# Three raw weight pieces requested two rounds later in an attention and feed-forward kernel

## The chip, the cores and the metric

The kernel runs on one core of one Trainium2 chip. The metric is the device time of one execution in microseconds (us); lower is better. The core has five engines with instruction streams of their own: TensorE (PE, matrix products), VectorE (DVE), ScalarE (ACT), GpSimd (POOL) and SyncE (SP), which here only issues DMA transfers. 16 DMA engines move the data. An engine takes its instructions in the order in which they were written.

## The reference

An attention with a threshold, followed by a feed-forward layer with a softmax-weighted activation and a layer norm:

```python
# q, k, v: (8, 8, 576, 64) float32; tau: a number
scores = matmul(q, k^T) / sqrt(64)
thresh = max(scores, -1) - tau
scores = where(scores >= thresh, scores, -1e9)
attn   = softmax(scores)                     # with 1e-9 in the sum
x      = matmul(attn, v), heads side by side # (4608, 512)
# w_in: (512, 1024), w_out: (1024, 512): float64; g_ln: (1024): float32
h    = x @ w_in
solu = h * softmax(h)
ln   = (solu - mean) / sqrt(var + 1e-6) * g_ln
out  = ln @ w_out                            # (4608, 512) float32
```

w_in and w_out arrive as 8-byte floats. The kernel reads them as pairs of 32-bit words and builds 4-byte floats from them itself.

## The kernel before, in words

**Rounds.** The loop at the end of the kernel runs in rounds (`rnd`), one for each of 144 slots, and some more to finish. A slot is half of a pair of heads. In the round of slot s, PE computes the scores (`s_ps`, L400), DVE takes the row maximum and a masked copy (`maxes`, L421, giving `nth`), and ACT applies the threshold ramp (L436) and the exponential (L445). One round later POOL normalises (L452 to L455), and DVE transposes the weights block by block into `T` (L467, in `blocks`). After every second slot, SP issues three DMAs that move `T` to `wT` (L476 and twice L478). Some rounds later PE multiplies `wT` by v (`pv`, L508) and ACT copies the result into `xh` (L538). When four pairs of heads are ready, PE multiplies `xh` by w_in (`h_ps`, L571), DVE takes the row maximum (`hm`, L586), and so on through the layer norm to the product with w_out (`o_ps`, L676). The texts write wT5, wT7, wT9, wT11, wT13 for the `wT` of the unit whose second slot is 5, 7, 9, 11, 13.

The order on every engine is the order in which Python calls the instructions, without rearrangement.

**Weight pieces.** w_in and w_out are cut into 16 raw pieces of 128 rows x 512 columns x 8 bytes = 512 KB: 0 to 7 are w_in, 8 to 15 w_out. `weight_load` (L248) asks SP for one. Piece x is converted in round x - 1: `weight_e` takes the exponent bits (DVE L258, then ACT L263, and L266 for w_out), `weight_m` the mantissa bits (DVE L274), `weight_b` puts them together (DVE L290 and L295), `weight_c` multiplies on POOL (L305) a round later. `weight_e(x + 1)` and `weight_m(x + 1)` run in the round of piece x, so the first read of piece x + 1 falls there. `weight_d` (L313) asks SP for two transfers that swap halves of converted w_out pieces.

**Which buffer.** The list `RAW` gives each piece a buffer that is otherwise used later: pieces 6 and 12 share `xh2`, 7 and 13 `xh3`, 8 and 14 `uT`. A load into such a buffer waits until DVE has read the piece that lay in it.

**When a piece is asked for.** The table `ASK` says which load is issued behind the conversion of which piece:

```python
weight_b(x)
for y in ASK.get(x, ()):
    weight_load(y)
```

In each round this stands after `blocks`, so after that round's `wT` transfers on SP, and before `weight_d` and the loads in `load_at` (v, q and k of this and the next batch).

Of the kernel before, what the change touches and what calls it, by code (L numbers as in the profile page):

```python
# [20 lines left out]
def kernel(  # L21
# [216 lines left out]
    third = heads.tile([P, S], F32, tag="kT", name="third")[:, 0:512].bitcast(I32)  # L238

    RAW = ['xh2', 'xh3', 'uT', 'xh1', 'u', 'V', 'xh2', 'xh3', 'uT', 'xh1', 'u', 'V', 'xh2', 'xh3', 'uT', 'xh2']  # L240
    ASK = {0: [6], 1: [7], 2: [8], 3: [9], 4: [10], 5: [11], 6: [12], 7: [13], 8: [14], 12: [15]}

    def weight_load(x, queue=None):
        raw = work.tile(
            [P, 512], I64 if wide else F32, tag=RAW[x],
            bufs=1, name="raw"
        )
        (queue or nc.sync).dma_start(out=raw, in_=piece(x)[0])  # L248
        raws[x] = dict(raw=raw)
# [29 lines left out]
    def weight_b(x, part=2):  # L279
        d = raws[x]  # L280
        _, dst, unit = piece(x)
        if not wide:
            if part != 1:
                nc.vector.tensor_scalar(out=dst, in0=d["raw"], scalar1=unit, scalar2=None, op0=ALU.mult)
            return
        words = d["raw"].bitcast(I32).rearrange("p (n two) -> p n two", two=2)
        lo, hi = words[:, :, 0], words[:, :, 1]
        if part != 1:
            m = d["m"]
            nc.vector.scalar_tensor_tensor(  # L290
                out=dst, in0=lo.bitcast(U32), scalar=2.0**-32, in1=m, op0=ALU.mult, op1=ALU.add
            )
        if part != 0:
            e = d["e"]
            nc.vector.scalar_tensor_tensor(  # L295
                out=e, in0=hi, scalar=-(2**31), in1=e, op0=ALU.bitwise_and, op1=ALU.bitwise_xor
            )
# [477 lines left out]
    with tc.manual_schedule():  # L775
# [45 lines left out]
        while True:  # L821
# [145 lines left out]
            if rnd in pieces:  # L967
# [4 lines left out]
# [3 lines that stand above are left out]
# [43 lines left out]
```

## Time and profile before

| | |
|---|---|
| median of 3 runs | 853.83 us (853.14 to 856.76) |
| profiled execution | 854.08 us, of which the span is 852.3 us |
| PE busy | 818.3 us (96%) |
| DVE busy | 680.2 us (80%) |
| ACT busy | 572.2 us (67%) |
| POOL busy | 499.1 us (59%) |
| DMA | 168.54 MB, mean 198 GB/s |
| chain that ended last | PE 82%, DVE 5%, DMA 5%, ACT 3% |
| mean granted TensorE clock | 0.985 |

The profile is one execution. Busy times are shares of the whole span; a stage can be bound by another engine than the whole. "Idle before <- X" names what ended an engine's idle time. A matmul's end is modelled, so a busy PE is not PE at its peak. Issue instructions of DMAs are not counted as busy; the SP queue view lists them with the time each took to issue.

### The profile page before, as it was taken

How to read it: one execution, taken by the hardware profiler on the slowest of the kernel's cores; microseconds unless marked ns; L12 is line 12 of the kernel's file. 1: busy time of each engine (PE TensorE's matmuls, PEld its weight loads, DVE VectorE, ACT ScalarE, POOL GpSimd, SP SyncE). 2: the span in 40 equal slices, each digit the busy share in tenths (PEclk: the TensorE clock that was granted, in tenths of full speed). 3: DMA queues.
4: the chain of work that ended last, by engine and by line, in shares of the span. 5: the costliest groups of instructions: out<-in, count | busy, mean ns of one | idle time of the engine just before them, and what ended most of it. 6: DMA issues, size and time to landing. Idle time of an engine off the chain costs nothing.

```text
span 852.3 us, 36109 instructions
## 1 busy us (share of the span) xinstructions
PE 818.3 (96%) x15363; PEld 619.0 (73%) x15363; DVE 680.2 (80%) x1241; ACT 572.2 (67%) x1127; POOL 499.1 (59%) x945
## 2 busy tenths in 40 slices
PE   5769899999999999999999999999999999999997
PEld 4547678677677787666687777777777777777555
DVE  5999977889788888888788878888888888787361
ACT  5888876877676666666676666677666677775121
POOL 3888756665566656565566666565666655555120
PEclk9779999999999999999999999999999999999999
DMA  9999887898888788887888887887889877655212
GB/s 332 271 252 220 214 217 202 209 240 211 220 220 215 192 200 209 214 211 180 206 234 208 198 182 196 231 211 196 191 225 226 207 183 187 156 136 139 66 38 63
DMA packets 75314, 168.54 MB, mean 198 GB/s; under 512 B 11146, under 2 KB 32658, under 8 KB 75154
## 3 DMA queue, kind: packets, MB, share of 16 engines
q1 hardware_dynamic: 74866, 165.82, 77.2%
q8 instruction: 120, 1.97, 1.0%
q10 hardware_dynamic: 288, 0.43, 0.2%
q14 instruction: 40, 0.33, 0.1%
HBM read 46.14 MB, written 9.44 MB: 65 GB/s over the span
## 4 chain that ended last, share of the span: by engine, by line
PE 82%; DVE 5%; DMA 5%; ACT 3%; issue 2%; POOL 1%; SPq 1%; DVEq 0%; ACTq 0%; POOLq 0%
PE o_ps L676 27%; PE h_ps L571 23%; PE s_ps L400 15%; PE pv L508 14%; DMA wT<-T 3%; PE h_ps L561 3%; DVE w L421 2%; DVE T L467 1%; ACT w L436 1%; ACT w L445 1%; DMA raw<-in_moe_w_in_dram 1%; DVE w L290 0%; POOL w L455 0%; SPq L478 0%; POOL sm L453 0%
## 5 line engine op out<-in xcount | busy, mean ns | idle before, releaser
L676 PE MATMUL o_ps<-w,uT 64*64 64x256 f32 x4608 | 269.3, 376 | 2.2 <-issue 1.9
L436 ACT ACTIVATE w<-s_ps,nth 128x576 f32<-128x576 f32 x280 | 196.9, 737 | 106.6 <-DVE nth L421 85.1
L676 PEld LDWEIGHTS o_ps<-w,uT 64*64 64x64 f32 x4608 | 226.8, 133 | 50.3 <-ACT xh L538 11.6
L421 DVE CUSTOM_DVE_ANT_0 w<-s_ps,tau_t 128x576 f32<-128x576 f32 x280 | 199.9, 750 | 77.6 <-PE s_ps L400 48.4
L455 POOL TENSOR_SCALAR w<-w,sm 128x576 f32<-128x576 f32 x288 | 221.9, 782 | 14.3
L467 DVE STREAM_TRANSPOSE T<-w 128x576 f32<-128x576 f32 x288 | 207.7, 755 | 22.7 <-POOL w L455 21.2
L571 PE MATMUL h_ps<-w,xh 64*64 64x512 f32 x1856 | 219.6, 589 | 0.0
L445 ACT ACTIVATE w<-w,ntau 128x576 f32<-128x576 f32 x288 | 219.5, 766 | 0.0
L508 PEld LDWEIGHTS pv<-wT,v 64*64 64x64 f32 x5760 | 170.5, 135 | 36.7 <-issue 22.2
L400 PE MATMUL s_ps<-kT,qT 64*64 64x64 f32 (+1 forms) x2048 | 173.6, 413 | 16.0 <-ACT w L436 13.5
L508 PE MATMUL pv<-wT,v 64*64 64x128 f32 (+1 forms) x5760 | 172.2, 262 | 5.0 <-DMA wT<-T 4.9
L571 PEld LDWEIGHTS h_ps<-w,xh 64*64 64x64 f32 x1856 | 113.0, 133 | 82.2 <-issue 54.4
L452 POOL TENSOR_SCALAR sm<-sm 128x2 f32<-128x2 f32 x144 | 36.1, 251 | 188.2 <-ACT w L445 184.8
L453 POOL TENSOR_TENSOR sm<-sm,mone 128x2 f32<-128x2 f32 x144 | 107.6, 747 | 12.0
L400 PEld LDWEIGHTS s_ps<-kT,qT 64*64 64x64 f32 x2048 | 71.5, 136 | 24.9 <-ACT w L436 18.5
L538 ACT COPY xh<-pv 128x256 f32<-128x256 f32 x64 | 25.4, 396 | 74.6 <-PE pv L508 74.6
L637 ACT ACTIVATE V<-u,nb,rs 128x1024 f32<-128x1024 f32 x36 | 44.7, 1241 | 40.6 <-POOL nb L627 34.4
L663 DVE STREAM_TRANSPOSE uT<-V 128x1024 f32<-128x1024 f32 x36 | 44.1, 1225 | 14.5 <-DMA V<-u 13.9
L445 ACT ACTIVATION_READ_ACCUMULATOR w<-w,ntau 128x1 f32 x288 | 55.3, 192 | 0.0
L601 DVE TENSOR_TENSOR u<-h_ps,u 128x1024 f32<-128x1024 f32 x36 | 42.8, 1190 | 9.9 <-ACT u L595 9.9
L642 DVE TENSOR_SCALAR u<-u,rs,nb 128x1024 f32<-128x1024 f32 x36 | 34.9, 969 | 17.5 <-ACT V L637 17.4
L595 ACT ACTIVATE u<-h_ps,hm 128x1024 f32<-128x1024 f32 x36 | 40.1, 1115 | 9.9 <-DMA V<-u 5.6
(81 smaller groups left out, 565.4 us busy)
## 6 DMA issues: line engine op xcount, KB each, us to landing
wT<-T SPq DMA_DIRECT2D x160, 288.0 KB, 6.5
wT<-T SPq DMA_DIRECT2D x64, 576.0 KB, 5.5
v<-in_v_dram SPq DMA_DIRECT2D x16, 576.0 KB, 4.9
V<-u SPq DMA_DIRECT2D x144, 64.0 KB, 3.5
out_dram<-ob SPq DMA_DIRECT2D x71, 128.0 KB, 2.7
q<-in_q_dram SPq DMA_DIRECT2D x28, 288.0 KB, 5.9
k<-in_k_dram SPq DMA_DIRECT2D x27, 288.0 KB, 6.1
qT<-flip SPq DMA_DIRECT2D x48, 144.0 KB, 3.4
```

The source lines that it names most:

```text
L400: nc.tensor.matmul(out=ps[h][ROWS[y], ks], lhsT=lhsT, rhs=d["kT"][ROWS[h], ks], start=True, stop=True,)
L421: nc.vector.tensor_tensor_reduce(out=w, in0=ps[:, 0:S], in1=(zero if loose else tau_t).to_broadcast([P, S]), scale=1.0, scalar=BIG, op0=AL ...
L436: nc.scalar.activation(out=d["w"][x], in_=d["w"][x] if d["loose"] else d["ps"][x][:, 0:S], func=AF.Prelu, bias=d["nth"][x], scale=-1.0, al ...
L445: nc.scalar.activation(out=w, in_=w, func=AF.Exp, bias=ntau, scale=1.0, accum_out=sm[:, x : x + 1])
L453: nc.gpsimd.tensor_tensor(out=sm, in0=sm, in1=mone, op=ALU.pow)
L455: nc.gpsimd.tensor_scalar(out=w, in0=w, scalar1=sm[:, x : x + 1], scalar2=1.0, op0=ALU.mult, op1=ALU.mult)
L467: nc.vector.transpose(out=T[:, :, r, h, :], in_=w)
L508: nc.tensor.matmul(out=to, lhsT=d["v"][ROWS[u], (h0 + h - u) % 4, m,], rhs=rhs, start=m == 0, stop=m == NK - 1,)
L571: mm = nc.tensor.matmul(out=h[ROWS[y], f], lhsT=x[ROWS[r], c, ROWS[y]], rhs=w1_parts[ROWS[r], c, part ^ r], start=part == 0 and c == 0, st ...
L637: nc.scalar.activation(out=V, in_=u, func=AF.Identity, bias=nb, scale=rs)
L663: nc.vector.transpose(out=uT, in_=d["V"].rearrange("p y (m x) -> p m y x", x=32))
L676: nc.tensor.matmul(out=d["o"][ROWS[z], 512 * (r ^ other) : 512 * (r ^ other) + 256], lhsT=d["uT"][ROWS[r], m].rearrange("p y x -> p (y x)" ...
```

## The change

Pieces 12, 13 and 14 are asked for behind the conversions of pieces 8, 9 and 10 (rounds 7, 8 and 9) instead of those of 6, 7 and 8 (rounds 5, 6 and 7). Their buffers, their conversions, the rounds of these and all other loads stay as they are.

```diff
-    ASK = {0: [6], 1: [7], 2: [8], 3: [9], 4: [10], 5: [11], 6: [12], 7: [13], 8: [14], 12: [15]}
+    ASK = {0: [6], 1: [7], 2: [8], 3: [9], 4: [10], 5: [11], 8: [12], 9: [13], 10: [14], 12: [15]}
```

The order of instructions on PE, DVE, ACT and POOL is the same in both kernels. On SP the order around the three loads changes from "11, 12, v, wT5, 13, 14, wT7" to "11, v, wT5, 12, wT7, 13, 14".

## Prediction, made before the changed kernel was run

> **What bounds the kernel now.** I read the page's 40 slices first: how full each engine is over the span. Each digit is the busy share of 21.3 us in tenths.
>
> ```profile
> PE   5769899999999999999999999999999999999997
> DVE  5999977889788888888788878888888888787361
> ```
>
> VectorE (DVE) is the full engine in slices 2 to 5 and TensorE (PE) from slice 6 on. The change works between 38 and 73 us. So I asked next for busy times by stage there; the columns are stage, length, busy us of PE, weight loads, DVE, ACT, POOL, then granted clock, DMA share, GB/s.
>
> ```profile
> 40.00:62.00 22.00, 13.63 (x208) 9.71 (x208) 21.28 (x45) 19.29 (x39) 18.22 (x24) 0.77 1.00 252
> 62.00:74.00 12.00, 11.12 (x170) 8.04 (x174) 11.54 (x24) 10.37 (x20) 10.91 (x16) 1.00 0.84 207
> 74.00:92.00 18.00, 17.05 (x386) 13.04 (x380) 17.78 (x34) 14.75 (x32) 15.56 (x24) 1.00 1.02 230
> ```
>
> DVE is idle for 0.72 us of the 22, 0.46 of the 12 and 0.22 of the 18: it sets the pace of all three stages, and the DMA engines are saturated beside it (1.00). Third, the chain of waits in time order, which says otherwise for ten microseconds:
>
> ```profile
> 55.38 7.90 DMA wT<-T
> ...
> 63.32 2.03 PE pv L508 x65
> ...
> 70.89 3.46 PE h_ps L571 x32
> 74.37 1.23 DVE hm L586
> ```
>
> The chain comes off DVE, through the transfer of the transposed weights wT of slots 6 and 7 (I write wT7), into PE, and back to DVE at 74.37. Fourth, SyncE's (SP's) queue, where the change is made: start, duration, line, transfer, count.
>
> ```profile
> 37.53 3.30 SPq L248 DMA_DIRECT2D raw<-in_moe_w_out_dram  x2
> 40.88 1.61 SPq L151 DMA_DIRECT2D v<-in_v_dram  x3
> 44.08 0.60 SPq L476 DMA_DIRECT2D wT<-T  x1
> ...
> 48.04 2.81 SPq L248 DMA_DIRECT2D raw<-in_moe_w_out_dram  x2
> 54.10 0.58 SPq L476 DMA_DIRECT2D wT<-T  x1
> 54.73 2.85 SPq L478 DMA_DIRECT2D wT<-T  x2
> 58.90 1.30 SPq L313 DMA_DIRECT2D w<-w  x2
> ...
> 64.16 0.60 SPq L476 DMA_DIRECT2D wT<-T  x1
> ```
>
> By the order in the code the pairs of L248 are pieces 11 and 12 (37.53 and 40.50), then 13 and 14 (48.04 and 50.52). Last, who needs what: PE's two pv groups, DVE's first reads of pieces 12, 13 and 14, and the DMA share per microsecond after wT of slots 8 and 9 (wT9).
>
> ```profile
> 62.20 0.44 PE L508 MATMUL pv<-wT,v 64*64 64x128 f32 x4 [2.48 <-DMA wT<-T]
> ...
> 73.95 2.23 PE L508 MATMUL pv<-wT,v 64*64 64x128 f32 x70
> ```
>
> ```profile
> 64.02 0.79 DVE L258 TENSOR_SCALAR em<-raw 128x512 int32<-128x512 int32 x1
> ...
> 69.04 0.68 DVE L258 TENSOR_SCALAR em<-raw 128x512 int32<-128x512 int32 x1
> ...
> 75.51 0.42 DVE L258 TENSOR_SCALAR third<-raw 128x512 int32<-128x512 int32 x1
> ```
>
> ```profile
> 70.00:71.00 1.00, 1.00 (x16) 0.61 (x11) 1.00 (x3) 0.97 (x4) 0.91 (x3) 1.00 0.33 78
> 71.00:72.00 1.00, 1.00 (x14) 0.64 (x10) 1.00 (x4) 0.48 (x1) 0.82 (x3) 1.00 0.10 20
> ```
>
> PE waits 2.48 us and then 0.68 for wT7; for wT9 it does not wait. At 70.4 the DMA backlog is gone, and the engines idle 0.67 + 0.90 = 1.57 us.
>
> **The change, part by part.** No compute instruction is added, removed or moved; three 512 KB loads stand later in SP's queue.
>
> *Where they go.* The order on SP becomes: piece 11, the v loads, wT5, piece 12, wT7, pieces 13 and 14, the weight shuffles of L313, the k loads, wT9. A moved load no longer waits for a conversion, since the piece whose buffer it takes was converted two rounds earlier. So 12 starts at about 48.04, 13 and 14 at 57.6 to 59.2, when SP is through with wT7 (54.73 + 2.85 = 57.58).
>
> *Pieces in time for DVE?* In this trace a raw piece lands 5.9 to 9.4 us after its issue (median 7.6). Piece 12: by 57.4, needed 64.02. Piece 13, issued by 58.2: 64 to 67.6, needed 69.04, at least 1.4 us to spare. Piece 14, issued by 59.2: by 68.6, needed 75.51. Cost 0; the cover of 13 is the thinnest, and each microsecond past 69.04 would be one of the kernel, since DVE is the pace.
>
> *SP's queue.* Behind 13 and 14 stand the shuffles, four k loads and wT9. SP now waits 58.90 - 57.58 = 1.32 us for POOL before the shuffles. Two issues of 0.33 to 0.97 each are 0.66 to 1.94, so the shuffles start 0 to 0.6 later; SP then has 1.01 us free between the k loads' end (60.24 + 2.91) and wT9 (64.16, released by DVE). Cost 0. The removed wait before 40.88 lets the v loads go about 2 us sooner; nobody waits for them.
>
> *wT7 sooner.* It no longer queues behind 13 and 14. Its last transfer took 7.90; the least of any wT before 120 us is 4.4, wT9's took 5.5 to 5.9. So it lands at 59.8 to 61.3 instead of 63.28; I take 60.5, near wT9's figure: 2.8 us. What of it reaches the end? PE's h_ps matmuls start sooner, but the second h_ps stands behind scores that wait for ACT, and ACT for DVE. DVE's step at 74.37 (hm) follows a transpose that ends at 72.77 + 1.50 = 74.27. Gain: 0.10 us; the rest turns into PE waiting for DVE. The most it could be is 0.46, all of DVE's idle time from 62 to 74.
>
> *wT9 later.* The bytes of 40 to 70 us are the same, so wT9 is later by the time the DMA engines run dry on the way. Taking 13 and 14 out of the queue before 54.10 removes 1.05 MB, at 252 GB/s 4.2 us of work. Piece 14, issued at 50.52 with the pair's 7.7, landed near 58.2, so 1.5 to 3.5 us of that work lay beyond 54.10 and was cover. Dry time: 0.7 to 2.7, I take 2.0, the upper half, because piece 12 goes alone. wT9 landed about 64.80 + 5.9 = 70.7; now 71.4 to 73.4, centre 72.7. PE's pv wants it at 73.95: 1.25 us to spare (0.55 to 2.55), and the scores behind that pv end 0.6 us before DVE wants them (76.03 + 1.23 against 77.86). Cost 0.
>
> [...]
>
> *Later on.* Of the 2.0 us, 1.57 fall into the trough at 70.4 to 72 and 0.63 into the one at 88 to 89 (share 0.37). wT11 (issued 76.87, its halves landing in 7.7) has 2 us to spare before its pv at 88.55. wT13 carries the chain at 95.80; it gets 0 to 0.5 later, I take 0.1. From 100 us on PE is full and the order unchanged: what is shifted stays shifted.
>
> Sum: -0.10 + 0.1 = 0. The profiled execution took 854.08 us (span 852.3 and 1.78 around it), 0.25 above the median of 853.83. I forecast the median, 853.9.
>
> **Rivals.**
>
> *Slower: the backlog moves to wT9.* If the queue of 4.5 MB between wT7 and wT9 (two raws, shuffles, k loads, both wT) drains at 207 GB/s, the row of 62 to 74, instead of 252, it takes 21.8 us from 54.7 and wT9 lands at 76.5. It decides beyond 74.55 (73.95 + 0.6): PE stands 2.5 us, DVE loses about 2, and wT13 is late too by up to 1: 856 to 857. For it: wT5 took 9.3 in its halves behind a raw and three v loads. Against: 207 contains the 1.57 us trough. If piece 13 is also late for 69.04, which would take 11 us, two more: about 859.
>
> *Faster: PE is the path from 63 to 74, as the chain says.* Then the 2.8 us of wT7 count: 851.0. For it: PE is full from 63.3 to 86. Against: DVE's own rows leave 0.46 us idle. DVE rows also stretch (0.79 for L258 against 0.42), and if these follow PE's timing, the gain could pass 4 us; little speaks for it.
>
> *A half-clock stretch falls elsewhere.* The granted clock was 0.50 from 54.6 to 58.0, after PE had idled from 49.7 to 52.4, and 1.00 after the like idle from 59.7 to 62.2. If such a 3.4 us falls onto h_ps at 65 to 74, PE loses 1.7 us and DVE's hm 1.6: 855.5. The change fills PE's idle time, which speaks against it. [...]
>
> The edit not doing what it says is excluded by the order on SP, which differs in just these loads.
>
> **How the numbers follow.** Forecast 0.62 (852.8 to 855.3: the bounds -0.46 and +0.5 and the spread of the runs); slower 0.20; faster 0.13; clock 0.05. About 0.5%, 4.3 us, is what a measurement of this kernel can tell from no change; nearly every case lies inside. Beyond it I put half of the slower case, 0.10, for two delays together, and 0.06 of the faster. Same 0.84. The range takes in the rivals' main prices and leaves out what lies beyond them: 851.0 to 857.4.
>
> **What would show it.** Right: wT7's pv starts near 60.5 with PE's wait of 2.48 gone or under 1; hm stays within 0.5 us of 74.37; DMA share dips between 51 and 55 and the trough at 71 shrinks; pv of wT9 shows no DMA wait. Wrong: hm near 72, or DVE idle before a read of raw at 69, or a pv at 74 to 96 waiting for wT a microsecond longer than now.

## The result and the profile after

The changed kernel is slower: a median of 858.07 us (854.79 to 866.6, 18 runs) beside 855.63 us (852.39 to 860.2, 18 runs) for the kernel before, run in turn with it. The two medians are 2.4 us apart; the ratio over all of these runs is 1.0045, with a 95% interval of 1.0026 to 1.0065, so about 3.9 us. Two executions among the experiments below, one of 1431.9 us and one of 984.3, ran at a far lower granted clock (0.56 and 0.85 over the whole execution) and are left out of the ratios given there. The forecast was 853.9 with 0.84 on "no change"; the measured median lies 0.7 us above the range. Part of that distance is the level: the three runs that the forecast started from had a median 1.8 us below the 855.63 of the eighteen.

Single executions of one kernel differ by more than the two kernels do, so one profile cannot show this loss by itself. The first profile of the changed kernel took 854.79 us with a span of 853.0, only 0.7 above the 852.3 of before. It still answers most of the steps of the prediction. First the busy share in 40 slices, which is nearly the same picture as before:

```profile
PE   6669899999999999999999999999999999999997
DVE  6999977889788888888788888888888888777361
```

Next the three stages (stage, length, busy us of PE, weight loads, DVE, ACT, POOL, then granted clock, DMA share, GB/s), and single microseconds with the same columns:

```profile
40.00:62.00 22.00, 14.35 (x232) 9.27 (x236) 20.91 (x44) 19.75 (x38) 18.71 (x24) 0.84 0.92 229
62.00:74.00 12.00, 12.00 (x164) 9.08 (x160) 10.24 (x21) 9.39 (x20) 9.52 (x14) 0.86 1.01 257
74.00:92.00 18.00, 16.99 (x384) 12.85 (x374) 17.80 (x34) 14.45 (x30) 15.69 (x25) 1.00 0.95 227
```

```profile
51.00:52.00 1.00, 0.65 (x10) 0.31 (x12) 1.00 (x2) 1.00 (x4) 1.00 (x2) 0.82 0.49 142
52.00:53.00 1.00, 1.00 (x10) 0.31 (x4) 1.00 (x3) 0.83 (x3) 0.85 (x2) 0.50 0.20 70
53.00:54.00 1.00, 1.00 (x24) 1.00 (x22) 1.00 (x3) 0.82 (x2) 0.92 (x2) 0.50 0.48 105
...
71.00:72.00 1.00, 1.00 (x16) 0.62 (x10) 1.00 (x4) 0.71 (x2) 0.90 (x2) 1.00 1.11 235
```

The DMA engines now run partly dry at 51 to 54 us (shares 0.49, 0.20 and 0.48), and the trough that lay at 71 to 72 (0.10 before) is full (1.11). DVE's loss in this profile is in the middle stage: 10.24 of 12 us busy, where it was 11.54. The clock there is 0.86, where it was 1.00. SP's queue shows the edit (start, duration, line, transfer, count):

```profile
46.04 0.93 SPq L248 DMA_DIRECT2D raw<-in_moe_w_out_dram  x1
52.40 0.57 SPq L476 DMA_DIRECT2D wT<-T  x1
53.02 2.92 SPq L478 DMA_DIRECT2D wT<-T  x2
55.98 2.05 SPq L248 DMA_DIRECT2D raw<-in_moe_w_out_dram  x2
...
59.47 3.68 SPq L142 DMA_DIRECT2D k<-in_k_dram  x4
63.27 0.60 SPq L476 DMA_DIRECT2D wT<-T  x1
64.83 1.89 SPq L478 DMA_DIRECT2D wT<-T  x2
```

Piece 12 goes alone at 46.04, pieces 13 and 14 at 55.98, behind wT7. The pv groups on PE, and two steps of DVE (start, duration, instruction, count, and in brackets the idle time ahead of it and what ended it):

```profile
60.03 0.44 PE L508 MATMUL pv<-wT,v 64*64 64x128 f32 x4 [2.01 <-DMA wT<-T]
61.36 3.44 PE L508 MATMUL pv<-wT,v 64*64 64x128 f32 x66 [0.90 <-DMA wT<-T]
...
73.66 2.22 PE L508 MATMUL pv<-wT,v 64*64 64x128 f32 x70
```

```profile
66.03 0.76 DVE L421 CUSTOM_DVE_ANT_0 w<-s_ps,tau_t 128x576 f32<-128x576 f32 x1 [1.32 <-PE s_ps L400]
...
74.07 1.22 DVE L586 TENSOR_REDUCE hm<-h_ps 128x1 f32<-128x1024 f32 x1
```

PE still waits for wT7, 2.01 + 0.90 us, though the two raw pieces are behind it now. Its pv then took 3.44 us at half clock (0.50 granted from 62 to 65 us) instead of 2.07, and DVE waited 1.32 us for the scores behind it. At wT9 (73.66) PE does not wait in this execution. The hm of DVE is 0.30 us sooner than before, but this execution was further ahead earlier: DVE's step on slot 4 starts at 28.98 us here and at 30.71 in the profile of before.

**The second profile of the changed kernel shows the loss** (861.79 us, span 860.0). Its chain of waits in time order, SP's queue, then PE and DVE:

```profile
59.29 7.58 DMA w<-w
66.86 0.02 issue
66.88 9.87 DMA wT<-T
76.75 0.04 issue
76.79 2.82 PE pv L508 x65
```

```profile
57.34 1.85 SPq L248 DMA_DIRECT2D raw<-in_moe_w_out_dram  x2
59.29 1.30 SPq L313 DMA_DIRECT2D w<-w  x2
...
65.97 2.09 SPq L478 DMA_DIRECT2D wT<-T  x2
```

```profile
75.42 0.44 PE L508 MATMUL pv<-wT,v 64*64 64x128 f32 x4 [1.72 <-DMA wT<-T]
76.79 2.91 PE L508 MATMUL pv<-wT,v 64*64 64x128 f32 x66 [0.94 <-DMA wT<-T]
```

```profile
81.47 0.76 DVE L421 CUSTOM_DVE_ANT_0 w<-s_ps,tau_t 128x576 f32<-128x576 f32 x1 [4.62 <-PE s_ps L400]
```

Read from the end: DVE stands still for 4.62 us at the scores of slot 13. They stand on PE behind a pv that waited 1.72 + 0.94 us for wT9. wT9's last transfer was issued at 66.88 and took 9.87 us. In the profile of before it is the second of the two transfers in this line:

```profile
64.80 2.93 SPq L478 DMA_DIRECT2D wT<-T  x2
```

There it was issued at 65.45 and took 6.30. (A transfer has landed when the last of its 16 semaphore increments is on record; landing times below are read from these.) The trace puts the issue at 66.88 behind the landing of a shuffle (w<-w), itself 7.58 us in flight behind pieces 13 and 14. wT9 does not read that shuffle. What ties the two is a semaphore: SP's 696 transfers use eight semaphores in turn, and none was issued before the eighth ahead of it had landed. The first profiles of before and after show that for 685 of 688 transfers each, and of the other three not all 16 increments are on record. The eighth ahead of wT9's last transfer is this shuffle, in both kernels; it landed at 66.86 here, 0.02 us ahead of the issue, and at 64.34 in the first profile of before, 1.11 ahead.

### The profile page after: what moved, and what is told of

The parts are those of the page before. It is cut to its first block, busy times and chain, and to the rows that moved or that the text cites. A ratio compares the mean times of both kernels' runs of the same rounds, so it can differ in the third digit from the quotient of the medians.

```text
span 853.0 us, 36106 instructions
## 1 busy us (share of the span) xinstructions
PE 818.4 (96%) x15363; PEld 622.5 (73%) x15363; DVE 680.4 (80%) x1241; ACT 572.6 (67%) x1127; POOL 500.1 (59%) x945
## 4 chain that ended last, share of the span: by engine, by line
PE 80%; DMA 5%; DVE 4%; ACT 3%; POOL 3%; SPq 2%; issue 2%; DVEq 0%; ACTq 0%; POOLq 0%
PE o_ps L676 27%; PE h_ps L571 22%; PE s_ps L400 15%; PE pv L508 14%; PE h_ps L561 3%; DMA wT<-T 3%; DVE w L421 1%; ACT w L436 1%; DMA q<-in_q_dram 1%; ACT w L445 1%; DVE T L467 1%; SPq L478 1%; POOL w L455 1%; DMA raw<-in_moe_w_in_dram 1%; SPq L483 1%
## 5 line engine op out<-in xcount | busy, mean ns | idle before, releaser
L421 DVE CUSTOM_DVE_ANT_0 w<-s_ps,tau_t 128x576 f32<-128x576 f32 x280 | 200.0, 750 | 75.6 <-PE s_ps L400 48.2
L571 PEld LDWEIGHTS h_ps<-w,xh 64*64 64x64 f32 x1856 | 116.5, 133 | 79.0 <-issue 51.8
L586 DVE TENSOR_REDUCE hm<-h_ps 128x1 f32<-128x1024 f32 x36 | 42.9, 1193 | 4.8 <-PE h_ps L561 2.7
```

Of the source, the lines that this page charges most:

```text
L421: nc.vector.tensor_tensor_reduce(out=w, in0=ps[:, 0:S], in1=(zero if loose else tau_t).to_broadcast([P, S]), scale=1.0, scalar=BIG, op0=AL ...
L571: mm = nc.tensor.matmul(out=h[ROWS[y], f], lhsT=x[ROWS[r], c, ROWS[y]], rhs=w1_parts[ROWS[r], c, part ^ r], start=part == 0 and c == 0, st ...
```

## Experiments

**Theories.** The first: pieces 13 and 14, now in the queue between wT7 and wT9, make wT9 late. Rivals: the dry stretch at 52 to 54 costs the time; piece 12 alone does it; a half-clock stretch on PE falls elsewhere, as the first profile suggests. In the expectations Q, and from the second profile on Q9, is the first theory, and C is the half clock.

**The changed kernel again** (no edit), for a second profile (shown above) and more runs.

> The changed kernel once more, for a second profiled execution and a ratio on this chip. Two theories of the 2 to 4 us that it loses. Q (queue): pieces 13 and 14, now behind wT7, share the DMA engines with wT7 and push wT9 and all behind it back; every execution pays, and the profile shows the scores of slots 11 to 20 late against DVE whatever the clock did. C (clock): a half-clock stretch falls onto pv of slots 6 and 7 and the scores behind it, and DVE waits 1 to 2 us there; it depends on where the clock's windows lie, so some executions pay and some do not. Both expect a ratio of 1.002 to 1.007. Q expects a DVE wait at round 11 in this profile too; C expects one only if the granted clock is 0.50 between about 60 and 66 us.

Measured: 859.54 us, ratio 1.0041 [1.0014, 1.0068]. The loss repeats, and here it stands at wT9. Q had expected a wait of DVE at slot 11 too; there it waits for nothing longer than 0.8 us in this profile.

**Parts of the change.**

```diff
-... 8: [12], 9: [13], 10: [14], 12: [15]}
+... 6: [12], 9: [13], 10: [14], 12: [15]}     # only 13 and 14 later
+... 7: [13], 8: [12, 14], 12: [15]}           # only 12 later
```

> Piece 12 goes back behind the conversion of piece 6; 13 and 14 stay behind those of 9 and 10, after wT7. Q expects nearly the whole loss, ratio 1.003 to 1.005 (+2.5 to +4 us). C expects about the same spread of times as the changed kernel, since pv of slots 6 and 7 still comes at the same time, ratio 1.001 to 1.005. If the loss came from piece 12 alone, the ratio is 1.000.

> Pieces 13 and 14 go back behind the conversions of 7 and 8, before wT7; only piece 12 stays behind that of piece 8, so that 13, 12 and 14 stand ahead of wT7. Q expects wT7 about 2 us later than before and wT9 as before: +0.5 to +2 us, ratio 1.0005 to 1.0025. C expects a later pv of slots 6 and 7 and hence a longer idle stretch of PE ahead of it, so more half-clock stretches, +1 to +4 us. If the order of the pieces does not matter, the ratio is 1.000.

Measured: 13 and 14 alone 860.19, 1.0038 [1.0007, 1.0069]; 12 alone 856.38, 1.0016 [0.9987, 1.0046]. The loss of 13 and 14 alone is clear and as large as that of the whole change; that of 12 alone cannot be told from none. The intervals overlap, so a small share of piece 12 is not excluded. The profiles agree: with 13 and 14 alone wT9 lands at 75.00 us and PE waits for it; with 12 alone it lands at 71.00 and PE does not. The first of the two, its chain and PE:

```profile
66.47 8.53 DMA wT<-T
```

```profile
75.04 2.07 PE L508 MATMUL pv<-wT,v 64*64 64x128 f32 x66 [0.71 <-DMA wT<-T]
```

**Without the three loads.** The conversions read what lies in the old buffers; the DMA engines are dry at 52 to 54 us here too (shares 0.02 and 0.36).

```diff
+        if x in (12, 13, 14):
+            raws[x] = dict(raw=kept[x - 6])
+            return
```

> Pieces 12, 13 and 14 are not loaded at all: their conversions read the raw pieces 6, 7 and 8 that still lie in the buffers, so half of w_out's rows there are wrong; every other instruction stays. 1.57 MB less to move between 40 and 66 us. Q expects that the loads cost the kernel before something too: 1 to 3 us faster than before, ratio 0.9965 to 0.999. C expects about the time of before, ratio 0.999 to 1.001, as DVE sets the pace there.

Measured: 856.12, 1.0001 [0.9975, 1.0027]. Its PE rows (line 514 is line 508 of the kernel before):

```profile
59.76 0.44 PE L514 MATMUL pv<-wT,v 64*64 64x128 f32 x4 [1.52 <-DMA wT<-T]
60.42 2.07 PE L514 MATMUL pv<-wT,v 64*64 64x128 f32 x66 [0.22 <-DMA wT<-T]
```

With no raw piece around it wT7 lets pv start at 60.42, and the kernel gains nothing clear by that; the 1 to 3 us that Q expected are missing. Nor does it clearly lose by the dry stretch (the interval ends at 0.27%, the loss of the change is 0.45%). What costs is the loads' new place, not their absence from the old one. wT9 lands at 70.66 here.

**Relief for wT9: the k loads behind it,** in the changed kernel and, as a control, in the one before.

```diff
-    for i, at, nm in ((NP, 9, "k"), ...
+    for i, at, nm in ((NP, 10, "k"), ...
```

> The changed kernel with the four k loads of the next batch asked for in round 10 instead of 9, so behind wT9 instead of ahead of it: 0.59 MB, some 2.4 us at 250 GB/s, less in front of wT9. Two theories after the second profile, where pv of slots 8 and 9 waited 1.72 and 0.94 us for wT9. Q9: the loss is wT9, late because two raw pieces now stand in the queue ahead of it; taking the k loads away gives that time back, ratio 0.999 to 1.002, and no pv wait at 74 to 77 us. C: the loss is the half-clock stretch at pv of slots 6 and 7 (61 to 65 us); wT9 does not matter, ratio 1.003 to 1.006.

> The same shift of the k loads in the kernel before, as a control, and as a candidate for a faster kernel. Q9: wT9 was in time there, so no change, ratio 0.9985 to 1.001. If k behind wT9 is itself too late for its transposes near 80 us, slower here and in the other: 1.001 to 1.004. C: no change.

Measured: 857.84, 1.0016 [0.9993, 1.004] and 857.65, 1.0019 [0.9996, 1.0041]. With the k loads out of the way no difference between the two kernels is left, within about 2.4 us, and PE's wait for wT9 is 0.26 us in the profile of the changed one. wT9's last transfer still took 8.96 us there, but it was issued at 64.43 and landed at 73.39: in that profile the relief is in the issue. Late k loads may cost 0.2% of their own, so this is no better version.

**More profiles of both kernels** (no edit), to count where each loses.

> The kernel before, for another profiled execution. Q9: wT9 lands before its pv, no wait at 74 us; no jump of more than 1 us between rounds 12 and 13. C: if the clock is 0.50 at 61 to 65 us here too and DVE waits 1 to 1.5 us at round 11, the clock is no part of the difference.

> As the run before it, a third profiled execution of the kernel before; the same expectations.

> The changed kernel, for a third profiled execution. Q9: wT9 lands between 73 and 77 us, against a pv that wants it at 73.7; a wait of 0 to 3 us. C: a DVE wait of 1 to 1.5 us at round 11 if the clock is 0.50 at 61 to 65 us.

> The changed kernel, a fourth profiled execution. Q9: the last transfer of wT9 is issued after a shuffle has landed, at 66 us or later, and its pv waits 1 to 3 us, as in two of three; without that wait the execution loses less than 2 us between rounds 4 and 18.

> The kernel before, a fourth profiled execution, for the count: no wait of the pv of slots 8 and 9 for wT9, as in the three so far; a loss of 0 to 2 us between rounds 4 and 18, set by the clock alone.

> The changed kernel, a fifth profiled execution, for the count: wT9 late in two of the four so far. If late, PE waits 2 to 3 us at 74 to 78 us and the loss between rounds 4 and 18 is 4 to 7 us; if not, 1 to 2 us.

With the first two these are four profiles of before and five of after. The first column of times runs from DVE's step on the scores of slot 4 (first L421) to that of slot 18, the second from slot 18 to slot 143; the third is PE's wait in sum for wT9; the last two are the issue and the landing of wT9's last transfer.

| profile | 4 to 18, us | 18 to 143, us | wait for wT9, us | wT9's last issue, us | landed, us |
|---|---|---|---|---|---|
| before 1 | 73.22 | 674.25 | 0 | 65.45 | 71.76 |
| before 2 | 75.23 | 675.36 | 0 | 67.15 | 71.73 |
| before 3 | 75.21 | 675.44 | 0 | 64.60 | 71.48 |
| before 4 | 74.03 | 674.91 | 0 | 63.53 | 70.30 |
| after 1 | 74.54 | 675.37 | 0 | 65.60 | 73.15 |
| after 2 | 78.58 | 677.15 | 2.66 | 66.88 | 76.75 |
| after 3 | 79.52 | 674.82 | 2.49 | 68.42 | 77.58 |
| after 4 | 74.73 | 678.60 | 0 | 65.97 | 74.47 |
| after 5 | 78.66 | 675.43 | 2.34 | 66.44 | 74.50 |

PE waits for wT9 in three of five executions after and in none of four before. wT9 itself lands later in all five: at 73.2 to 77.6 us, against 70.3 to 71.8 before. In the two without a wait it came just in time (after 1: 0.51 us ahead of pv; after 4: 0.18 behind the first of pv's matmuls), so the expectation that the fourth would wait was missed narrowly. The profiles of the edited kernels split in the same way: 70.7 to 71.2 in the four with nothing added between wT7 and wT9, 73.4 to 80.0 in the five with two pieces or two extra loads there (the kernels with spare matmuls aside). Where PE does not wait, the changed kernel takes 74.5 and 74.7 us to slot 18, as the one before does (73.2 to 75.2). Where it waits, 78.6 to 79.5. The mean rises by 2.8 us, from 74.4 to 77.2. The mean over all timed runs of the study rises by 3.0, from 856.33 (126 runs of before) to 859.32 (33 of after). The third and the fifth profile of after, on PE:

```profile
76.27 0.44 PE L508 MATMUL pv<-wT,v 64*64 64x128 f32 x4 [1.57 <-DMA wT<-T]
77.63 2.07 PE L508 MATMUL pv<-wT,v 64*64 64x128 f32 x66 [0.92 <-DMA wT<-T]
```

```profile
73.50 0.44 PE L508 MATMUL pv<-wT,v 64*64 64x128 f32 x4 [1.73 <-DMA wT<-T]
74.55 3.74 PE L508 MATMUL pv<-wT,v 64*64 64x128 f32 x66 [0.61 <-DMA wT<-T]
```

The lateness alone cost DVE 2.31 us at slot 13 in the third, where pv ran at its usual 2.07. In the fifth and the second PE's wait was followed by half clock (0.50 granted at 76 to 78 us and at 78 to 81; pv 3.74 and 2.91), and DVE lost 3.68 and 4.62. Of the 4.5 us by which these three exceed the mean of before, 2.6 lie ahead of the step on slot 13 and 1.9 behind it, up to slot 18; what the second part is made of was not followed.

The half clock that the first profile of after suffers at slot 11 (0.50 granted; DVE waits 1.32) is not the difference: DVE waits 2.02 at slot 10 in before 2, 1.98 at slot 11 in before 3, and 0.91 in before 4.

**Extra transfers in the kernel before,** two of 512 KB: where the change puts 13 and 14 (behind the conversions of 9 and 10), or behind the k loads, just ahead of wT9.

```diff
+                if x in (9, 10):
+                    extra = work.tile([P, 512], I64, tag=RAW[x], bufs=1, name="extra")
+                    nc.sync.dma_start(out=extra, in_=piece(x + 4)[0])
```

```diff
+            if rnd == 9:
+                for tag, y in (("xh1", 13), ("u", 14)):
+                    extra = work.tile([P, 512], I64, tag=tag, bufs=1, name="extra")
+                    nc.sync.dma_start(out=extra, in_=piece(y)[0])
```

> The kernel before, with pieces 12, 13 and 14 asked for where they were, and two more loads of 512 KB (the rows of pieces 13 and 14 once more, into buffers that nobody reads until later) behind wT7 at the two places where the changed kernel asks for 13 and 14. Q9: the bytes ahead of wT9 are the cause, so the loss comes without moving any piece: ratio 1.002 to 1.006, pv of slots 8 and 9 waits for wT9 in some executions. C, or a cause in the stretch at 52 to 55 us where the DMA engines run dry in the changed kernel: there is no dry stretch here and wT7 stands behind the same queue as before, so ratio 0.999 to 1.001.

> The kernel before with two more loads of 512 KB, now behind the k loads and just ahead of wT9, issued at about 63 us, when wT7 lands; so wT7 stays as it was and only wT9 gets 1.05 MB, 4.2 us at 250 GB/s, in front of it. Q9: wT9 lands near 75 us instead of 70.7, its pv waits 1 us or more, ratio 1.002 to 1.005. If instead the harm is done at wT7 (raw pieces that run beside it, then the clock), ratio 0.999 to 1.0015 and no wait at the pv of slots 8 and 9.

Measured: 860.26, 1.0034 [1.0005, 1.0063], and 858.83, 1.0021 [0.9995, 1.0048]. The first is slower by nearly as much as the change, but its one profile lost the time earlier than expected, at wT7. Its chain, and PE:

```profile
53.88 12.60 DMA wT<-T
```

```profile
65.43 0.69 PE L508 MATMUL pv<-wT,v 64*64 64x128 f32 x4 [2.64 <-DMA wT<-T]
66.52 3.89 PE L508 MATMUL pv<-wT,v 64*64 64x128 f32 x66 [0.40 <-DMA wT<-T]
```

wT7's last transfer took 12.60 us and DVE waited 4.90 at slot 11. PE did not wait for wT9. The extra loads are not shown to have done this: they were asked for from 57.50 us on, and wT5's last two transfers, which had landed by 57.28, had already taken 11.66 and 12.07 us (8.75 and 9.35 in the first profile of before). So 1 MB more between wT7 and wT9 does cost over the twelve runs, but this profile does not show where. The second is inconclusive: its interval holds 1, and its profile lost 1.49 us to half clock (0.50 granted at 65 to 67 us) at slot 11. wT9 landed at 76.03 there, later than in any profile of before; but pv, late itself, began only at 75.84, and PE did not wait.

**The shuffle behind wT9,** in both kernels, since the chain puts wT9's last issue behind one.

```diff
-            if rnd - 1 in pieces:
+            if rnd - 1 in pieces and rnd != 9:
                 weight_d(pieces[rnd - 1])
+            if rnd == 10:
+                weight_d(9)
```

> The changed kernel with the two 256 KB transfers that swap halves of w_out pieces 8 and 9 asked for one round later, behind wT9: 0.52 MB, 2.1 us, less ahead of wT9, and the last transfer of wT9 no longer waits for the first of them. Pieces 13 and 14 still run beside wT7. Q9: the loss is gone or nearly, ratio 0.999 to 1.002. If the harm is done at wT7, it stays: 1.003 to 1.006.

> The same in the kernel before, as the control. Both: ratio 0.9985 to 1.0005, since wT9 was in time there; if the shuffles beside wT7 had cost something there, up to 0.2% faster.

Measured: 857.82, 1.0016 [0.9992, 1.0041] and 856.19, 1.0006 [0.9984, 1.0028]. The changed kernel's loss is no longer clear, and PE's wait for wT9 is 0.73 us in the profile. But the same profile has the next long landing, of wT13, and PE waits 3.90 us for it:

```profile
88.43 10.03 DMA wT<-T
```

The shift of 0.1% between the two is below what these runs can tell. wT9's last transfer was issued at 65.03, no longer behind a shuffle, and still took 8.93 us: the issue is only a part of the lateness.

**A warm clock,** by 72 spare matmuls in each of rounds 4, 6, 8 and 10, into columns that nothing reads, so that PE's idle times would not be followed by half clock, as those before 61.88 us were in the first profile of after (0.50 from there to 65.29).

```diff
+            if rnd in (4, 6, 8, 10):
+                for n in range(18): ...   # h, y in 0, 1
+                    nc.tensor.matmul(out=live[rnd]["ps"][h][ROWS[y], 640:768], ...)
```

> The changed kernel with 72 spare 64 x 128 matmuls on the identity in each of rounds 4, 6, 8 and 10, into unused columns of the score banks, where PE stands idle for 2.0 to 2.7 us; they keep PE busy so that the clock stays up. C: without half-clock stretches between 48 and 66 us the loss is gone: within 0.1% of the kernel before with the same spare matmuls. Q9: the loss stays, +1.5 to +4 us against that kernel; pv at 74 to 77 us still waits for wT9 in some executions.

> The kernel before with the same spare matmuls, the partner of the run above. Both theories: ratio 0.997 to 1.001, a gain if half-clock stretches cost the kernel before something, none if DVE hides them.

Measured: 869.61, 1.0157 [1.0132, 1.0182] and 870.67, 1.017 [1.0148, 1.0193]. The edit was too blunt. The spare work took 5 to 7 us a round and became the bound, the granted clock was 0.77 to 1.00 in the three stages read (54 to 58, 58 to 62 and 82 to 86 us of the changed kernel), and in the changed kernel the DMA engines stood nearly idle where they should have been crowded. One stage of its profile (columns as above):

```profile
54.00:58.00 4.00, 1.76 (x38) 0.74 (x26) 4.00 (x9) 3.97 (x10) 1.49 (x2) 1.00 0.06 18
```

With the round lengthened, PE waits for no wT and the change costs nothing that these few runs could tell (the difference is -1.1 us, plus or minus 2.0), which fits the first theory. Of the clock it says nothing.

## Why the prediction was wrong

**The step that failed** is "wT9 later", priced at "Cost 0". The mechanism was seen, and stands in the prediction as the slower rival at 0.20; the sizes were off. The prediction had wT9 land at 71.4 to 73.4 against a need of 73.95. It landed at 74.5, 76.8 and 77.6 in the three executions where PE waited (the fifth, second and third profile, in this order below too). Three terms of that step were too small:

- *Start.* The prediction let wT9 land at 64.80 + 5.9 = 70.7 before the change. That is the second of its three transfers. The last, issued at 65.45, landed at 71.76. With that figure its own 2.0 us of delay gives 73.8, and the margin of 1.25 us is 0.2.
- *Landing.* The prediction added only the time that the DMA engines run dry. The last transfer took 8.1, 9.9 and 9.2 us in those three, and 8.6 in the mean of five, against 6.1 in the mean of four before. Before, wT9 ran into an emptying queue (the trough at 71); now 1 MB more is ahead of it and the trough is full.
- *Issue.* The prediction let SP issue wT9 as before, its "SP's queue … Cost 0". In the late executions the last issue comes at 66.4, 66.9 and 68.4 us, against 65.45 in the first profile of before. In four of the five profiles of after, and in that of 13 and 14 alone, it comes 0.01 to 0.02 us behind the landing of a shuffle, the eighth transfer ahead of it (landed at 65.59, 66.86, 68.40, 66.42 and 66.45 us); in the first profile of before it comes 1.11 us behind. The prediction counted what SP has to issue, not what must have landed first. One of the four before issued at 67.15 and was still in time, so the issue alone does not decide; the terms together do.

Over the means, wT9 lands 4.0 us later instead of 2.0: 1.5 by a later issue and 2.5 by a longer landing.

The dry time itself was about as forecast in the first profile: 1.8 us of idle share between 51 and 54 (0.51 + 0.80 + 0.52), against 2.0. But it does not set wT9's lateness: over the five profiles it is 0.4 to 2.9 (50 to 55 us), and wT9 is latest (77.6) in the one with 0.4. The traces show the issue and the landing behind other transfers, not the dry time, to be what grew.

Two smaller figures of the prediction do not come out either: 1.57 and 0.63 are 2.2, not the 2.0 that they divide, and the least time of a raw piece is 4.75 us (the one asked for at 70.99), not 5.9. The result does not hang on them.

**wT7 sooner: too much.** Forecast 60.5, gain 2.8 us; pv's long group starts at 61.36 in the first profile, and PE's wait is not gone. Over five profiles of after its mean start is 61.4, over four of before 62.9: 1.5 us. wT7's last transfer took 6.5 us in the mean (4.9 to 9.0) instead of 8.4, where the prediction had reckoned with 4.4 to 5.9. It took 6.5 also in the run without loads, so the two pieces that now stand behind it are not shown to slow it.

**Right.** No raw piece was late for DVE: its reads of 12, 13 and 14 start at 62.33, 68.75 and 75.21 in the first profile, none with a wait for a load. The earlier wT7 brings nothing that shows (the run without loads has 1.0001): the chain's path over PE was not what set the pace, and the faster rival falls. The dip at 51 to 55 and the vanished trough came as described, and the first profile shows no wait at wT9, as forecast; but that was luck of one execution: wT9's landing varies from 73.2 to 77.6 us over five, far more than the margin of 1.25.

**The rivals.** *The backlog moves to wT9* is what happened, at 2.3 to 4.6 us of DVE for each late execution instead of "about 2", since PE's wait can be followed by half clock, a combination that no case had. *Half clock elsewhere* occurs in both kernels and explains no difference by itself.

**What stays open.** That wT9 is later is shown by every profile. That its lateness carries the loss rests on the count of three in five against none in four, on the parts of the change, and on the k loads' relief; the extra transfers agree in time, but their one profile lost its time at wT7. How far other places share the loss over many executions isn't settled, nor is why wT9's landing varies so much from one execution to the next. Nor is whether the later part of the span takes a share: 18 to 143 has means of 675.0 before and 676.3 after, within which single executions differ by up to 3.8 us. No kernel tried was faster than the one before: the nearest are the shuffle behind wT9 in it (1.0006) and the one that leaves the loads out.

## What to carry to other kernels

A load moved later in a shared queue is charged to whatever stands behind it: price the next consumer with landing times measured behind a full queue (here 7.6 to 9.9 us), not with its own time behind an emptying one (4.6 to 6.9), and take the last of its transfers, not the one before. Look also at what an issue itself must wait for: with eight semaphores in turn, the slow shuffle here (7.58 us, landed at 66.86) held back the eighth transfer behind it (issued at 66.88), which does not need its data. A margin smaller than the spread of landing times is no cover, and a cost of zero there should be a chance of paying the whole wait. When the expected effect is below 1% and executions differ by as much, count a stage over several profiles before believing what one of them shows.

## What the runs showed of the hardware

- With 1 MB more ahead of it on the queue a transfer took longer to land: wT9's last one, of 288 KB, 4.6 to 6.9 us in the four profiles of before and 7.6 to 9.9 in the five of after. In the first profiles of before and after the transfers of SP whose landing is on record, 692 of 696 in each, landed in the order of their issue.
- In the first profiles of before and after each stretch of one granted clock, but the first and the last, lasts a multiple of 3.41 us (3.41 to 791.89 us). From 35 to 830 us the clock fell to 0.50 behind each of the five full-clock steps (a stretch cut into parts of 3.41 us) in which PE was idle for 1.77 to 2.81 us, and behind none of the 455 in which it was idle for 1.71 or less (PE's busy time as the trace models it). How the idle time falls on the steps made the difference there: before, PE's waits of 2.48 and 0.68 us for wT7 lay in two steps (58.02 to 61.43 and 61.43 to 64.84 us), idle for 1.71 and 1.45 in all, and the clock stayed at 1.00; after, those of 2.01 and 0.90 lay in one (58.47 to 61.88), idle for 2.46, and it fell to 0.50. At wT9, PE waits of 1.73 and 0.61 us with 0.44 of work between were followed by half clock (after 5), and waits of 1.57 and 0.92 were not (after 3, 1.00 from 72 to 83 us). The two stretches, after 5 and after 3, with the columns as above:

```profile
76.00:78.00 2.00, 2.00 (x47) 2.00 (x44) 0.00 (x0) 0.00 (x0) 2.00 (x3) 0.50 1.05 260
```

```profile
78.00:79.50 1.50, 1.50 (x65) 1.50 (x61) 0.32 (x1) 0.00 (x0) 1.50 (x3) 1.00 1.05 244
```
